# DCN-v2 cross layers on one core: 1024-row superblocks in 128x32 column tiles, the 32 leftover features packed four deep, and DMA transposes inside

## Chip, cores, metric

One core of a Trainium2 chip. The metric is the device time of one execution in microseconds (us), as a median over executions. The span, which the profile covers, runs from the first to the last instruction; the time is longer than the span. Engines are named as in the profile: PE is TensorE, PEld its weight loads, DVE VectorE, ACT ScalarE, POOL GpSimd, SP SyncE (it issues most of the DMAs here). "L200" is line 200 of the kernel in question.

## The reference

```python
B, D, L = 4096, 416, 6            # x0 [B, D], ws [L, D, D], bs [L, D], all bf16
def reference(x0, ws, bs):
    x = x0
    for l in range(L):
        x = x0 * (x @ ws[l] + bs[l]) + x
    return x
```

Every layer result is x0 times something: x_l = x0 * (1 + the sum of all earlier x @ w + b). Both kernels use this. PSUM keeps accumulating over the layers, the sum of the biases is prepared once (`cb_sb`), and an eviction is one instruction: (PSUM + bias) * x0. The width is 416 = 3 x 128 + 32, and the 32 leftover features are the awkward part.

## The kernel before

x0 is held transposed (features on partitions). Rows come in blocks of 512, two blocks (a pair) at a time, each with four PSUM banks. Per block and layer, TensorE does 12 full-array matmuls (4 output chunks x 3 input chunks, 512 columns each) and four 32-row tiles for the leftover input features. The leftover features are replicated four times, so the fourth output chunk is 128 columns wide like the other three (all 576 matmuls of L200 are `128*128` in the trace) but holds only 32 distinct results.

```python
for p in range(NPAIR):                       # 4 pairs of 512-row blocks
    emit_inT(p, 0)                           # 16 PE transposes of x0 per block into the block's own banks
    if p > 0:
        emit_inT(p, 1)
    for l in range(L):
        for par in range(2):
            ...                              # waits cut
            for m in range(NCH):             # NCH = 4 output chunks, the fourth is the leftover, 4 copies
                for k in range(3):
                    pe.matmul(ps[:, 4 * par + m, :],
                              lhsT=w_sb[:, l, k, m * 128:(m + 1) * 128],
                              rhs=src[:, k, cols], ...)
            for m in range(NCH):             # leftover input: four 32-row tiles side by side
                ins = pe.matmul(ps[:, 4 * par + m, :],
                                lhsT=w3_sb[32 * m:32 * m + 32, l, :],
                                rhs=src[32 * m:32 * m + 32, 3, cols],
                                tile_position=(32 * m, 0), ...)
            ins.then_inc(s_mm[par], 1)
    for par in range(2):
        pe.wait_ge(s_x[par], p * L + L)      # last layer evicted
        ...                                  # 16 PE transposes back per block, then ScalarE copies, then the store
# VectorE, per block and layer: four times
dve.scalar_tensor_tensor(out=xT_sb[:, c, cols], in0=ps[:, 4 * par + c, :],
                         scalar=cb_sb[:, c, l:l + 1], in1=x0T_sb[:, c, cols],
                         op0=ALU.add, op1=ALU.mult)
```

## Time and profile before

| | before |
|---|---|
| time, median of 2 runs | 199.01 us (198.84 to 199.18) |
| span of the profiled execution | 193.8 us |
| PE busy / DVE busy | 174.1 us / 130.8 us |
| one 512-row block and layer | 3.02 us (6.05 us per 1024 rows) |
| turn between two pairs | 9.2, 8.3 and 8.5 us |

In all the profile blocks below, rows of the view left out between two shown are marked by "...". The page of before: busy time and its share of the span, then two rows in 40 slices of the span (tenths of a slice that PE was busy, and tenths of full clock granted to it), and the chain of work that ended last, by engine.

```profile
PE 174.1 (90%) x1028; PEld 78.4 (40%) x1028; DVE 130.8 (68%) x192; ACT 31.8 (16%) x69; POOL 11.6 (6%) x50
...
PE   0595999999799999999969999999978999999971
...
PEclk9999999999958999999987999999997999999995
...
PE 84%; ACT 6%; DVE 5%; DMA 1%; issue 1%; SPq 1%; DVEq 0%; ACTq 0%
```

TensorE is the bound, and there are three dips, at which its granted clock falls too. The chain of before in order of time (start us, length us, what) has one of them in full:

```profile
46.79 2.70 PE ps L200 x12
49.49 0.36 PE ps L209 x4
...
49.87 2.73 DVE xT_sb L245 x4
...
52.65 2.34 PE ps L226 x16
54.99 1.83 PE ps L171 x16
...
56.84 2.07 ACT x0T_sb L269 x4
...
59.05 2.87 PE ps L200 x12
```

The regular part is 2.70 + 0.33 us. The turn, from 49.85 to 59.05, is a queue in which each step waits for the one before: last evictions, transposes out, transposes in, copies. Over 49 to 60 us the clock granted was 0.69; in the regular part it was 1.00.

### The profile page before, as it was taken

Reading aid. Unit: us, or ns where it says so; the run is one execution under the profiler, and the core shown is the slowest. Engines: PE = TensorE matmul, PEld = TensorE weight load, DVE = VectorE, ACT = ScalarE, POOL = GpSimd, SP = SyncE. Lnnn points to the kernel's source line nnn. Section 1 sums busy time; section 2 is a strip of 40 time slices with the busy share of each in tenths; the row PEclk is TensorE's granted clock in tenths of the full one; section 3 lists DMA queues with packets and bytes.
Section 4 is the critical chain, followed back from the end, with each engine's and each line's share of the span. In section 5 each row is a group of like instructions: output and inputs, shape, how many; then the busy total and the mean of one; then the engine's idle time right before and its main releaser. Section 6 shows DMA issues by size and latency. Waiting matters only on the chain.

```text
span 193.8 us, 2464 instructions
## 1 busy us (share of the span) xinstructions
PE 174.1 (90%) x1028; PEld 78.4 (40%) x1028; DVE 130.8 (68%) x192; ACT 31.8 (16%) x69; POOL 11.6 (6%) x50
## 2 busy tenths in 40 slices
PE   0595999999799999999969999999978999999971
PEld 0342434334374343433455434334356343343440
DVE  0023889898701988989820889898850698988970
ACT  2503000000365000000078000000049000000033
POOL 4176400000000000000000000000000000000000
PEclk9999999999958999999987999999997999999995
DMA  4699400000031000000022000000013000000005
GB/s 131 159 364 354 133 0 3 0 0 3 0 116 60 5 0 0 0 0 3 0 88 90 3 0 0 0 0 3 0 61 115 0 3 0 2 0 0 3 0 176
DMA packets 12411, 9.09 MB, mean 47 GB/s; under 512 B 1898, under 2 KB 12400, under 8 KB 12400
## 3 DMA queue, kind: packets, MB, share of 16 engines
q1 hardware_dynamic: 12400, 8.94, 14.7%
q8 instruction: 8, 0.13, 0.3%
q14 instruction: 3, 0.02, 0.0%
HBM read 5.53 MB, written 3.41 MB: 46 GB/s over the span
## 4 chain that ended last, share of the span: by engine, by line
PE 84%; ACT 6%; DVE 5%; DMA 1%; issue 1%; SPq 1%; DVEq 0%; ACTq 0%
PE ps L200 68%; PE ps L209 8%; DVE xT_sb L245 5%; PE ps L171 4%; ACT x0T_sb L269 4%; PE ps L226 4%; ACT o_sb L279 2%; DMA bsa_sb<-in_bs_dram 1%; DVEq L33 0%; SPq L73 0%; SPq L71 0%; SPq L70 0%; ACTq L33 0%; PE ps L154 0%
## 5 line engine op out<-in xcount | busy, mean ns | idle before, releaser
L245 DVE SCALAR_TENSOR_TENSOR xT_sb<-ps,cb_sb,x0T_sb 128x512 bf16<-128x512 f32 x192 | 130.8, 744 | 57.0 <-PE ps L209 57.0
L200 PE MATMUL ps<-xT_sb,w_sb 128*128 128x512 bf16 x480 | 110.6, 380 | 0.0
L200 PEld LDWEIGHTS ps<-xT_sb,w_sb 128*128 128x128 bf16 x480 | 43.7, 98 | 56.3 <-DVE xT_sb L245 6.8
L279 ACT ACTIVATE o_sb<-ps 128x416 bf16<-128x416 bf16 x32 | 14.0, 522 | 148.8 <-PE ps L226 148.8
L200 PE MATMUL ps<-x0T_sb,w_sb 128*128 128x512 bf16 x96 | 23.5, 397 | 5.2 <-ACT x0T_sb L269 5.1
L226 PE MATMUL ps<-ident,xT_sb 128*128 128x128 bf16 (+1 forms) x128 | 13.9, 223 | 5.1 <-DVE xT_sb L245 5.1
L269 ACT ACTIVATE x0T_sb<-ps 128x512 bf16<-128x512 bf16 x32 | 16.4, 613 | 7.2 <-PE ps L171 7.0
L200 PEld LDWEIGHTS ps<-x0T_sb,w_sb 128*128 128x128 bf16 x96 | 9.1, 101 | 17.4 <-issue 8.8
L209 PE MATMUL ps<-xT_sb,w_sb 32*128 32x512 bf16 x160 | 15.8, 384 | 0.0
L171 PE MATMUL ps<-ident,xin_sb 128*128 128x128 bf16 x128 | 13.7, 293 | 0.7 <-ACT o_sb L279 0.4
L226 PEld LDWEIGHTS ps<-ident,xT_sb 128*128 128x128 bf16 (+1 forms) x128 | 8.7, 99 | 10.8 <-DVE xT_sb L245 6.4
L171 PEld LDWEIGHTS ps<-ident,xin_sb 128*128 128x128 bf16 x128 | 11.9, 136 | 1.7 <-issue 1.6
L209 PEld LDWEIGHTS ps<-xT_sb,w_sb 32*128 32x128 bf16 x160 | 4.0, 90 | 17.0 <-issue 17.0
L132 POOL COPY xin_sb<-xin_sb 128x128 bf16<-128x128 bf16 x24 | 6.2, 296 | 8.2 <-DMA xin_sb<-in_x_dram 8.2
L154 PE MATMUL ps<-u_sb,bsa_sb 7*128 7x6 bf16 x4 | 0.2, 162 | 4.6 <-DMA bsa_sb<-in_bs_dram 4.6
L141 POOL COPY w_sb<-w_sb 128x96 bf16<-128x96 bf16 x18 | 4.1, 270 | 2.3 <-DMA w_sb<-in_ws_dram 2.1
L209 PE MATMUL ps<-x0T_sb,w_sb 32*128 32x512 bf16 x32 | 3.2, 384 | 0.0
L209 PEld LDWEIGHTS ps<-x0T_sb,w_sb 32*128 32x128 bf16 x32 | 0.8, 90 | 3.4 <-issue 3.4
L154 PEld LDWEIGHTS ps<-u_sb,bsa_sb 7*128 7x128 bf16 x4 | 0.2, 99 | 4.5 <-issue 4.5
L259 ACT ACT_TABLE_LOAD x1 | 1.3, 1283 | 0.8 <-PEq L298 0.8
L259 ACT ACTIVATE cb_sb<-ps 128x6 f32<-128x6 f32 x4 | 0.4, 181 | 2.8 <-PE ps L154 2.8
L118 POOL MEMSET bsa_sb<- 1x512 bf16 x1 | 0.5, 518 | 0.0
(7 smaller groups left out, 1.1 us busy)
## 6 DMA issues: line engine op xcount, KB each, us to landing
xin_sb<-in_x_dram SPq DMA_DIRECT2D x8, 416.0 KB, 7.0
out_dram<-o_sb SPq DMA_DIRECT2D x7, 416.0 KB, 2.7
w_sb<-in_ws_dram SPq DMA_DIRECT2D x6, 312.0 KB, 4.5
out_dram<-o_sb SPq DMA_DIRECT2D x4, 104.0 KB, 1.8
w_sb<-in_ws_dram SPq DMA_DIRECT2D x3, 48.0 KB, 2.5
w_sb<-in_ws_dram SPq DMA_DIRECT2D x4, 12.0 KB, 1.8
bsa_sb<-in_bs_dram SPq DMA_DIRECT2D x3, 0.4 KB
bsa_sb<-in_bs_dram SPq DMA_DIRECT2D x1, 4.9 KB
```

The lines of the kernel that those rows point to most:

```text
L118: pool.memset(bsa_sb[0:1, :], 1.0).then_inc(s_setup, 1)
L132: pool.tensor_copy(out=xin_sb[:, p * SUB:(p + 1) * SUB, DF + r * DR:DF + (r + 1) * DR], in_=xin_sb[:, p * SUB:(p + 1) * SUB, DF:D],).then_ ...
L141: pool.tensor_copy(out=w_sb[:, l, :, DF + r * DR:DF + (r + 1) * DR], in_=w_sb[:, l, :, DF:D],).then_inc(s_wr[l], 1)
L154: ins = pe.matmul(ps[:, 7, c * 8:c * 8 + L], lhsT=bsa_sb[:, c * 128:(c + 1) * 128], rhs=u_sb[:, :], start=True, stop=True,)
L171: ins = pe.transpose(out=psT[:, 4 * par + c, j * 128:(j + 1) * 128], in_=xin_sb[:, blk * SUB + j, c * 128:(c + 1) * 128], identity=ident[: ...
L200: pe.matmul(ps[:, 4 * par + m, :], lhsT=w_sb[:, l, k, m * 128:(m + 1) * 128], rhs=src[:, k, cols], start=(l == 0 and k == 0), stop=False, ...
L209: ins = pe.matmul(ps[:, 4 * par + m, :], lhsT=w3_sb[32 * m:32 * m + 32, l, :], rhs=src[32 * m:32 * m + 32, 3, cols], start=False, stop=Tru ...
L226: ins = pe.transpose(out=psT[:, 4 * par + j, c * 128:c * 128 + fw], in_=xT_sb[0:fw, c, b0:b0 + 128], identity=ident[0:fw, 0:fw],)
L245: ins = dve.scalar_tensor_tensor(out=xT_sb[:, c, cols], in0=ps[:, 4 * par + c, :], scalar=cb_sb[:, c, l:l + 1], in1=x0T_sb[:, c, cols], op ...
L259: ins = act.activation(out=cb_sb[:, c, :], in_=ps[:, 7, c * 8:c * 8 + L], func=ACTF.Copy)
L269: ins = act.activation(out=x0T_sb[:, c, cols], in_=psT[:, 4 * par + c, 0:NB], func=ACTF.Copy,)
L279: ins = act.activation(out=o_sb[:, blk * SUB + j, :], in_=psT[:, 4 * par + j, 0:D], func=ACTF.Copy,)
```

## The change

The intent is threefold. Pack the leftover so that TensorE streams less: its output in four row groups, side by side in four column tiles. Make the turns vanish: inner superblocks get their transposed input from DMA and give their output to DMA. Take the leftover's eviction off VectorE. Everything except the leftover's input runs in 128x32 column tiles, so that the array changes its tiling only twice per layer. The core of it, cut:

```diff
-    NB = 512
+    SB = 1024
+    NS = B // SB
+    H = SB // 2
+    G = SB // 4
+    TAIL, SPARE = 6, 7
 ...
+            # SP: input of superblocks 1 to 3, output of superblocks 0 to 2
+            for s in range(1, NS):
+                sp.dma_start_transpose(
+                    x0T_sb[:, :, s * SB:(s + 1) * SB], x0[s * SB:(s + 1) * SB, 0:DF]
+                ).then_inc(s_x0T[s], 16)
+            for s in range(NS - 1):
 ...
+                for c in range(NC):
+                    sp.dma_start_transpose(
+                        o_sb[:, s * JS:(s + 1) * JS, c * 128:(c + 1) * 128], xo_sb[:, s, c, :]
+                    ).then_inc(s_oT, 16)
+                sp.wait_ge(s_xt, n)
+                sp.dma_start_transpose(ot_sb[:, s, :, :], xot_sb[:, s, :]).then_inc(s_ot, 16)
 ...
+            # PE: the main product of a half (512 rows), 3 x 3 groups of four column tiles
+                                for q in range(4):
+                                    f0 = m * 128 + 32 * q
+                                    ins = tile_mm(
+                                        ps[32 * q:32 * q + 32, NC * half + m, :],
+                                        w_sb[:, l, k, f0:f0 + 32], src[:, k, o:o + H], q,
+                                        l == 0 and k == 0 and half == 0, True,
+                                    )
 ...
+            # PE: main(0, ...), then the leftover's input in row tiles; row groups g share banks in pairs; the batches keep two of one bank apart
+                    for i, jobs in enumerate((
+                        ((0, 0), (1, 1), (2, 0), (3, 1)), ((0, 2), (2, 2)),
+                        ((0, 1), (1, 0), (2, 1), (3, 0)), ((1, 2), (3, 2)),
+                    )):
+                        if i >= 2:
+                            pe.wait_ge(s_row, 3 * n + i - 1)
 ...
+            # PE: the leftover's output, one 256-row group per column tile, then main(1, None)
+                    for k in range(NC):
+                        for g in range(4):
+                            tile_mm(
+                                ps[32 * g:32 * g + 32, TAIL, 0:G], w_sb[:, l, k, DF:D],
+                                src[:, k, off + g * G:off + (g + 1) * G], g, l == 0 and k == 0, True,
+                            )
 ...
+            # ACT, then POOL: the leftover's eviction and product
+                    act.activation(
+                        out=t32_sb[:, n % 2, :], in_=ps[:, TAIL, 0:G], func=ACTF.Identity,
+                        bias=cb_sb[:, NC, l:l + 1],
+                    ).then_inc(s_ta, 1)
+                    pool.tensor_tensor(
+                        out=dst, in0=t32_sb[:, n % 2, :], in1=x0t_sb[:, s, :], op=ALU.mult
+                    ).then_inc(s_xt, 1)
```

In all, the first half superblock is still transposed by TensorE, as is the output of the last superblock. Twenty filler matmuls at the start are meant to bring TensorE to its full rate before the first product (in after they do not: its groups start 0.427 us apart, later ones 0.216; see run 9).

## The prediction

> **What bounds before.** TensorE. The chain of waits is 84% PE; the table of busy time has PE 90% (174.1 us), DVE 68% (130.8 us). The timeline shows a steady rhythm: each 512-row block and layer takes 3.02 us (12 full-array matmuls 2.70 us, then four 32-row tiles 0.33 us for 32 leftover features), so 6.05 us per 1024 rows, 145 us for 48. DVE fits inside (four evictions 2.73 us, 0.683 us apart). The rest of the chain is not rhythm: three block-pair turns of about 9 us each (49.9 to 59.1: last eviction, 32 transposes, ScalarE copies, nothing overlapping), about 27 us; start to the first main matmul 8.9 us; end after the last matmul 8.7 us (185.1 to 193.8). Time minus span is 5.2 us.
>
> **What the change does, per 1024 rows and layer.**
> - Main product: 18 groups of four 128x32 tiles, 512 columns. If the four run together, 18 x 0.216 = 3.89 us (0.216: the twelve matmuls, 2.70 us, less about 0.11 us for the mode switch; an estimate).
> - Leftover input in four row tiles at N=256, ordered in four batches, two of which wait for earlier ones. Estimate 0.71 us, from the 0.384 us of one 512-column tile less half its streaming, about 0.28 us, plus 0.43 us of queueing.[...]
> - Leftover output packed by four row groups in column tiles: 16 matmuls of 256 columns, four deep, about 0.43 us.
> - PE sum 5.2 us against 6.05. DVE: 6 evictions instead of 8, 6 x 0.683 = 4.1 us; the loop DVE, then ordered row tiles, then DVE is 4.1 + 0.75 + about 0.2 = 5.05 us, nearly a tie. The leftover's eviction moves to ScalarE (about 0.5 us) and GpSimd (estimate 0.6-1.2 us, from 0.296 us for a 128-wide copy); its result is due about 4 us later, so hidden. Rhythm: 5.3 us; 24 x 5.3 = 127 us. Gain 18 us.
> - Turns: input and output transposes of the inner superblocks go to DMA, and the next superblock's first layer depends on nothing just finished. Gain about 27 us, nearly all on the critical path.
> - Start and end remain: first layer done at about 14.5 us; end about 6.3 us.
>
> 14.5 + 23 x 5.3 + 6.3 = 143 us of span, + 5.2 = 148; I add 4 us for stalls in the first layers. **Predicted 152 us, range 143 to 168.** Faster by over 2%: 0.93; within: 0.04; slower: 0.03.
>
> **What shows each step.** Right: groups of four tiles 0.21-0.23 us apart in the timeline; rhythm per layer 5.2-5.5 us; no PE gap over 0.5 us at superblock borders; GpSimd never the releaser of PE; DVE busy about 105 us; final part 6-7 us.
>
> **What would make it wrong.**
> - [...]If weight loads of small tiles stop hiding[...].
> - DMA transposes slow: under about 60 GB/s (estimate, 851 KB in 14 us) the GpSimd tail copy waits and stalls the tail, and the first transpose delays layers 0 and 1.
> - Evictions at 0.744 us each instead of 0.683, plus slower ordered tiles: rhythm 5.7 us, 160 us.

The sum of 5.2 us for TensorE came from 3.89 + 0.43 us and 0.85 to 0.9 us for the row tiles. The last had, on top of the 0.71 us that the text derives, 0.14 to 0.19 us for a change of mode; that came to 5.17 to 5.22 us. The term is cut, as no trace showed it in that form, and the terms still printed make 5.03 us.

## The result, and the profile after

| | before | after |
|---|---|---|
| time, median of 2 runs | 199.01 us | 141.44 us (141.40, 141.47) |
| span of the profiled execution | 193.8 us | 138.9 us |
| PE / DVE busy | 174.1 / 130.8 us | 131.3 / 98.7 us |
| 1024 rows and one layer | 6.05 us | 5.13 us |
| turns | 26.0 us in all | none |

The ratio is 0.713, with a 95% interval of 0.704 to 0.722. Ratios here are the mean time of one kernel's runs over that of the other's of the same rounds, so they are not quite the ratio of the medians quoted (for this first result the two medians give 0.711). Executions over 1.5% slower than the fastest of the same kernel are left out of the means. The direction was forecast; the time lies 1.6 us under the lower end of the range.

The page of after, the same lines as of before:

```profile
PE 131.3 (94%) x2506; PEld 67.2 (48%) x2506; DVE 98.7 (71%) x149; ACT 17.7 (13%) x36; POOL 21.1 (15%) x44
...
PE   6799999999999999999999999999999999999950
...
PEclk9999999999999999999999999999999999999995
...
PE 90%; DVE 3%; DMA 3%; ACT 1%; SPq 0%; issue 0%
```

The dips are gone and so are those of the clock. The chain of after in order of time, from the first main product into the second layer, and across the border of superblocks 0 and 1 (the row tiles at 36.76 are those of superblock 0's last layer, at 41.89 those of superblock 1's first):

```profile
6.08 4.08 PE ps L174 x33
...
10.18 0.39 ACT x0t_sb L377
...
10.71 0.76 PE ps L272 x12
11.47 4.43 PE ps L174 x88
...
36.76 0.69 PE ps L272 x12
37.45 4.43 PE ps L174 x88
41.89 0.69 PE ps L272 x12
```

The border cannot be told from the rest: 4.43 + 0.69 us, layer after layer, with no wait between (in layers 2 to 4 of superblock 0 the first is 4.55 us, because eight transposes of the next leftover inputs run there). The timeline of one layer (start, length, engine, line, operation, shapes, count, and in brackets the idle time before it):

```profile
62.33 0.76 PE L272 MATMUL ps<-xt_sb,wt_sb 32*128 32x256 bf16 x12
...
63.02 0.51 PE L174 MATMUL ps<-xT_sb,w_sb 128*32 128x256 bf16 x12
63.13 4.04 DVE L348 SCALAR_TENSOR_TENSOR xT_sb<-ps,cb_sb,x0T_sb 128x512 bf16<-128x512 f32 x6 [1.09 <-PE ps L272]
...
63.36 0.28 PE L174 MATMUL ps<-xt_sb,wc_sb 128*32 128x256 bf16 x4
...
63.47 4.06 PE L174 MATMUL ps<-xT_sb,w_sb 128*32 128x512 bf16 x72
63.70 0.47 ACT L387 ACTIVATE t_sb<-ps,cb_sb 128x256 f32<-128x256 f32 x1 [4.65 <-PE ps L174]
64.25 0.67 POOL L158 TENSOR_TENSOR xt_sb<-t_sb,x0t_sb 128x256 bf16<-128x256 f32 x1 [4.46 <-ACT t_sb L387]
...
67.46 0.76 PE L272 MATMUL ps<-xt_sb,wt_sb 32*128 32x256 bf16 x12
```

Row tiles start at 62.33 and again at 67.46: the rhythm is 5.13 us. The leftover's result leaves GpSimd at 64.92 and is due at 67.46. VectorE finishes its six evictions at 67.17, only 0.29 us before the row tiles that must wait for it. In the single instructions of the trace, the groups of four 512-column tiles start 0.216 us apart, those of 256 columns 0.11 us.

Where the 54.9 us of span went, by subtraction on the two chains: turns 26.0 us (9.20 + 8.31 + 8.46); rhythm 24 x (6.05 - 5.13) = 22.1 us. The remaining 6.8 us are start and end (first products, and the second block's transposes and copies in the middle of the first pair of before).

### The profile page after: what moved, and what is told of

The parts are those of the page before. It is cut to its first block, busy times and chain, and to the rows that moved or that the text cites. A ratio compares the mean times of both kernels' runs of the same rounds, so it can differ in the third digit from the quotient of the medians.

```text
span 138.9 us, 5386 instructions
## 1 busy us (share of the span) xinstructions
PE 131.3 (94%) x2506; PEld 67.2 (48%) x2506; DVE 98.7 (71%) x149; ACT 17.7 (13%) x36; POOL 21.1 (15%) x44
## 4 chain that ended last, share of the span: by engine, by line
PE 90%; DVE 3%; DMA 3%; ACT 1%; SPq 0%; issue 0%
PE ps L174 77%; PE ps L272 12%; DVE xo_sb L348 3%; DMA xin_sb<-in_x_dram 3%; PE ps L312 1%; PE ps L198 1%; ACT o_sb L403 1%; SPq L90 0%; ACT x0t_sb L377 0%
## 5 line engine op out<-in xcount | busy, mean ns | idle before, releaser
L348 DVE SCALAR_TENSOR_TENSOR xT_sb<-ps,cb_sb,x0T_sb 128x512 bf16<-128x512 f32 x120 | 80.9, 743 | 26.1 <-PE ps L272 26.1
L174 PE MATMUL ps<-xT_sb,w_sb 128*32 128x512 bf16 (+1 forms) x1680 | 91.1, 364 | 0.0
L174 PEld LDWEIGHTS ps<-xT_sb,w_sb 128*32 128x32 bf16 x1680 | 42.9, 97 | 37.2
L158 POOL TENSOR_TENSOR xt_sb<-t_sb,x0t_sb 128x256 bf16<-128x256 f32 x20 | 13.5, 674 | 86.3 <-ACT t_sb L387 86.3
L387 ACT ACTIVATE t_sb<-ps,cb_sb 128x256 f32<-128x256 f32 x24 | 11.4, 474 | 103.0 <-PE ps L174 103.0
L174 PE MATMUL ps<-x0T_sb,w_sb 128*32 128x512 bf16 (+1 forms) x336 | 20.4, 389 | 0.0
L348 DVE SCALAR_TENSOR_TENSOR xo_sb<-ps,cb_sb,x0T_sb 128x512 bf16<-128x512 f32 x24 | 16.2, 744 | 4.3 <-PE ps L272 4.3
L272 PE MATMUL ps<-xt_sb,wt_sb 32*128 32x256 bf16 x240 | 15.2, 274 | 0.0
L174 PEld LDWEIGHTS ps<-x0T_sb,w_sb 128*32 128x32 bf16 x336 | 9.0, 101 | 8.4 <-issue 1.6
L158 POOL TENSOR_TENSOR xot_sb<-t_sb,x0t_sb 128x256 bf16<-128x256 f32 x4 | 2.7, 674 | 17.8 <-ACT t_sb L387 17.8
L198 PE MATMUL ps<-ident,xin_sb 128*128 128x128 bf16 x12 | 1.6, 305 | 1.1 <-DMA xin_sb<-in_x_dram 1.1
```

The lines of the kernel that those rows point to most:

```text
L158: pool.tensor_tensor(out=dst, in0=t32_sb[:, n % 2, :], in1=x0t_sb[:, s, :], op=ALU.mult).then_inc(s_xt, 1)
L174: return pe.matmul(dst, lhsT=lhsT, rhs=rhs, start=start, stop=stop, skip_group_check=True, tile_position=(0, 32 * q),)
L198: ins = pe.transpose(out=psT[:, NC * (1 - h) + c, (j % 2) * 128:(j % 2 + 1) * 128], in_=xin_sb[:, j, c * 128:(c + 1) * 128], identity=iden ...
L272: ins = pe.matmul(ps[:, NC * (g // 2) + m, (g % 2) * G:(g % 2) * G + G], lhsT=wt_sb[p, l, m * 128:(m + 1) * 128], rhs=srct[p, :], start=l ...
L348: dve.scalar_tensor_tensor(out=dst, in0=ps[:, NC * half + c, :], scalar=cb_sb[:, c, l:l + 1], in1=x0T_sb[:, c, o:o + H], op0=ALU.add, op1= ...
L387: act.activation(out=t32_sb[:, n % 2, :], in_=ps[:, TAIL, 0:G], func=ACTF.Identity, bias=cb_sb[:, NC, l:l + 1],).then_inc(s_ta, 1)
```

## Experiments

Two theories stood for each part. Mine was that streaming in TensorE is the whole of the rhythm, and that the leftover's packing, not the column tiles, shortened it; that the turns were removed whole; and that the prediction was high because of terms added for safety and for time outside the span. The rivals are named in each text.

The base is the changed kernel's 141.44 us, and for runs 6 to 12 its repetition in run 5 (runs 9 to 12 were in other rounds than run 5). Runs 1 to 4 were on one chip, 5 to 12 on another. "Expected" is the text before each run.

### 1. The main product in full-array matmuls again

```diff
-                                for q in range(4):
-                                    f0 = m * 128 + 32 * q
-                                    ins = tile_mm(ps[32 * q:32 * q + 32, NC * half + m, :],
-                                        w_sb[:, l, k, f0:f0 + 32], src[:, k, o:o + H], q, ...)
+                                ins = pe.matmul(ps[:, NC * half + m, :],
+                                    lhsT=w_sb[:, l, k, m * 128:(m + 1) * 128], rhs=src[:, k, o:o + H], ...)
```

> The changed kernel with the 18 main groups per layer as full 128x128 matmuls again, everything else kept. Theory (the gain of the rhythm is not from column tiles, they only save one mode switch per layer: column-row-column has two, full-row-column-full has three): rhythm 5.13 to about 5.25-5.35 us, time 141.4 to 144-147 us. Rival (small column tiles themselves stream faster, or their weight loads hide better): rhythm over 5.5 us, time over 150 us.[...]

Measured: 144.25 us (143.21 to 144.44). In its timeline the row tiles start at 63.25 and 68.48, a rhythm of 5.23 us:

```profile
63.25 0.76 PE L271 MATMUL ps<-xt_sb,wt_sb 32*128 32x256 bf16 x12
...
64.28 0.28 PE L174 MATMUL ps<-xt_sb,wc_sb 128*32 128x256 bf16 x4
64.49 3.57 PEld L228 LDWEIGHTS ps<-xT_sb,w_sb 128*128 128x128 bf16 x18 [0.21 <-issue]
64.49 4.06 PE L228 MATMUL ps<-xT_sb,w_sb 128*128 128x512 bf16 x18
...
68.48 0.76 PE L271 MATMUL ps<-xt_sb,wt_sb 32*128 32x256 bf16 x12
```

Eighteen full-array matmuls take 4.06 us, exactly what 72 column tiles take in the line of after. So four tiles abreast stream like one full matmul (0.216 us from one to the next in both traces), and their four weight loads stay hidden (in the layer of after at 63.36 the 72 loads are 3.67 us of PEld, over the 4.06 us of the matmuls). The 0.10 us per layer lies ahead of the full matmuls, where the array changes from column tiles to the whole: they start 0.21 us after the leftover's last group (64.28), while in after the same step takes 0.11 us (63.36 to 63.47). Avoiding that switch is worth 24 x 0.10 = 2.4 us of the 2.8 us that column tiles brought by the time (3.6 us by the median span, 142.25 against 138.65); the rest is not accounted for.

### 2. The kernel before, only its turns removed

```diff
+            for p in range(2, NBLK):                      # SP: blocks 2 to 7
+                sp.dma_start_transpose(x0T_sb[:, 0:3, p * NB:(p + 1) * NB], x0[p * NB:(p + 1) * NB, 0:DF])
+                sp.wait_ge(s_xr[p], 3)
+                sp.dma_start_transpose(x0T_sb[:, 3, ...], xrep_sb[:, p * SUB:(p + 1) * SUB, :] ...)
 ...                                                       # output of blocks 0 to 5 likewise, a GpSimd copy for the leftover
-                emit_inT(p, 0)
-                if p > 0:
-                    emit_inT(p, 1)
+                if p == 0:
+                    emit_inT(p, 0)
```

> The kernel before with one part of the change alone: its three inner turns use DMA transposes in and out (512-row blocks, full-array and 32-row matmuls, tail on VectorE all as before). Theory (the turns held 26 us of the critical path and DMA transposes take all of it away, the rhythm of 3.02 us is untouched): 199.0 to 172-175 us, no PE gap over 0.5 us at the block-pair borders. Rival (the turn gain needs the 1024-row superblocks, or DMA transposes bring waits of their own): over 180 us.

Measured: 172.36 us against 199.04 us in the same rounds, 26.7 us less, by the medians of all executions. Some of both kernels were slow; the fast ones alone have means of 170.85 and 197.85 us, 27.0 us less (ratio 0.864, 0.850 to 0.877). The chain of this run, across the border of its first two pairs (which begins at 53.99 with the second pair's first layer):

```profile
53.66 0.33 PE ps L250 x4
53.99 2.70 PE ps L241 x12
```

The turns are gone with 512-row blocks too, and the rhythm of 3.02 us is untouched. So this part alone is worth almost half the gain, and it needs neither superblocks nor tiles. It is the DMA transposes, and the fact that a pair's first layer then waits for nothing but its own banks.

### 3. The leftover's output unpacked

```diff
                         for g in range(4):
-                            tile_mm(ps[32 * g:32 * g + 32, TAIL, 0:G], ..., g, l == 0 and k == 0, True)
+                            for q in (range(4) if s > 0 else (g,)):
+                                tile_mm(ps[32 * q:32 * q + 32, TAIL if q == g else SPARE, 0:G], ..., q, ...)
```

> The changed kernel with the packing of the leftover output undone in 18 of the 24 layers (superblocks 1 to 3): each of the four 256-row groups again occupies all four column tiles, three of the four results go to an unused bank; result stays right. 36 more matmuls of 256 columns per layer, four abreast[...]. Theory (the rhythm is bound by streaming in TensorE, and the packing is nearly the whole 0.92 us that the rhythm gained): rhythm 5.13 to about 6.09 us in those layers, time 141.4 to about 158.7 us (157-160). Rival (slack elsewhere in the layer hides part of it): under 153 us.

Measured: 158.7 us (157.97 to 158.92), result right. The chain has 5.42 us where after has 4.43, again with the row tiles' 0.69:

```profile
60.27 5.42 PE ps L174 x124
65.69 0.69 PE ps L272 x12
```

That is 0.99 us more for 36 more matmuls, nine groups of four that start 0.11 us apart in the trace (the expected 6.09 us was 5.13 + 0.96 us for the nine); in 18 layers it makes 17.8 us by the rhythm, and 17.3 us were measured by the time. Nothing hides any of it. Before, the fourth output chunk streamed 2 x 3 x 512 columns per 1024 rows, of which this packing leaves 3 x 256; so the packing accounts for the 0.92 us of the rhythm, with what little the row tiles and the corner add and take.

### 4. The row tiles without their order (wrong result)

```diff
-                        ((0, 0), (1, 1), (2, 0), (3, 1)), ((0, 2), (2, 2)),
-                        ((0, 1), (1, 0), (2, 1), (3, 0)), ((1, 2), (3, 2)),
+                        ((0, 0), (1, 1), (2, 0), (3, 1)), ((0, 0), (1, 1), (2, 0), (3, 1)),
+                        ((0, 0), (1, 1), (2, 0), (3, 1)),
 ...
-                        if i >= 2:
-                            pe.wait_ge(s_row, 3 * n + i - 1)
```

> Wrong result on purpose: the twelve row-tile matmuls of the leftover input write one bank per row group, so that no two row groups share a bank and the two ordering waits go; three batches of four instead of four batches. Theory (the order costs time in every layer: 4 batches and a wait, 0.69 us from batch start to the next mode): 0.69 to about 0.43-0.50 us, time 141.4 to 135-137 us. Rival ([...]VectorE's loop takes over): over 140 us.

Measured: 135.78 us (135.33 to 136.12). In the chain the row tiles fall from 0.69 to 0.44 us:

```profile
55.48 4.44 PE ps L174 x88
59.92 0.44 PE ps L270 x12
```

So the order costs 0.25 us per layer, 5.7 us in all. The starts of the batches in the two traces divide it: in after the third batch starts 0.24 us after the second, here 0.11 us, so the first wait is about half; the other half is the fourth batch, which is 0.12 us after the third. The order is the largest thing left in the rhythm besides streaming. Whether the waits could go in the right kernel was not tried: that would take away the waits between row groups that share a bank, not the sharing, and no run shows what becomes of the result then. It stays open.

### 5. The changed kernel once more

> The changed kernel once more, on the same chip as the next three runs, as their base. All theories: 141-142.5 us; time minus span 2.0-2.8 us, as in every run so far, so that the 5.2 us taken in the prediction was the median of two runs set against the span of a faster run and not a fixed cost.

Measured: 141.54 us median (139.18 to 141.94, four runs). The times confirm the first ones. Time minus span was 1.98 to 3.34 us, wider than expected. For the kernel before, over the 25 executions of the three sets of rounds, it was 2.05 to 2.14 us, while the spans themselves went from 193.9 to 197.7 us. So the 193.8 us of the first profile was one of the shortest executions and the 199.01 us came from others: the 5.2 us were 2.1 us of fixed time and about 3.1 us of scatter between executions. Of this run's four executions the one of 139.18 us was labelled fast and the others slow, because they lie over 1.5% above it; their clocks (0.989 to 0.999, against 0.990) are at most 0.001 lower, and their spans, 138.6 to 138.8 us against 137.2, are those of the first runs. So they serve as the base: 141.54 us of time, 138.65 us of median span. By the labels alone the base would be the one execution of 139.18 us, runs 6 to 8 would stand 2.4 us further above it, and runs 9 to 12 (139.83, 139.47, 140.89 and 138.99 us) would gain nothing. So those small effects rest on what the traces show and not on the times. In most other runs time minus span was 1.7 to 2.0 us, so part of a difference in time from this base (mean 2.7 us) lies outside the span; for effects of about 1 us the span is the steadier measure, and both are given below.

### 6. The inner output transposes done twice

```diff
                 for c in range(NC):
+                    sp.dma_start_transpose(od_sb[:, c, :, :], xo_sb[:, s, c, :]).then_inc(s_oT, 16)
+                sp.wait_ge(s_oT, 32 * NC * s + 16 * NC)
+                for c in range(NC):
                     sp.dma_start_transpose(
```

> The changed kernel with every inner output DMA transpose done twice, one after the other (first into a scratch tile). Theory (the DMA transposes are wholly off the critical path, with several us to spare before GpSimd's copy is due): no change, within 0.5 us of the base. Rival (they are near the limit, as the prediction allowed with its 4 us for stalls): over 2 us slower, with PE waiting for GpSimd in the second or third layer of superblocks 1 to 3.

Measured: 141.92 us against 141.54; by median span 139.95 against 138.65. By the time it is within the expected 0.5 us (one of its four executions, 143.47 us, was slow; the fast ones are 141.28 to 141.96); by the span it is 1.3 us slower, so the theory's "no change" did not hold, and what the rival named, PE waiting for GpSimd, is seen, though the loss is 1.3 us and not over 2. The waits of this run (engine, line, waited for whom: us in total, times, longest) and its timeline after superblock 0 say how:

```profile
PE ps L278 <- POOL xt_sb L164: 1.3, 2, 1.1
```

```profile
56.79 0.40 POOL L172 COPY o_sb<-ot_sb 128x256 bf16<-128x256 bf16 x1 [7.76 <-DMA ot_sb<-xot_sb]
...
57.87 0.76 PE L278 MATMUL ps<-xt_sb,wt_sb 32*128 32x256 bf16 x12 [1.10 <-POOL xt_sb L164]
```

With twice the transposes the leftover lands at about 56.8, and PE waits 1.1 us. In the changed kernel its transpose is issued at 46.64 and lands 2.4 us later (the median of these), at about 49.0. It would be in time until about 55.7. The slack at this border is thus about 6.6 us (an estimate across two runs): the way of failure that the prediction named is real and is 6.6 us away. From the first issue (41.62) to this landing the DMA transposes of superblock 0's output in after (832 KB) went at some 115 GB/s (the prediction put its danger under about 60), and SP's four issues alone took 6.2 us of those 7.4; the transfer by itself was not measured.

### 7. The leftover on VectorE again

```diff
+                        if half == 1:                     # VectorE, between its two halves
+                            dve.wait_ge(s_to, n + 1)
+                            dve.scalar_tensor_tensor(out=..., in0=ps[:, TAIL, 0:G], scalar=cb_sb[:, NC, l:l + 1],
+                                in1=x0t_sb[:, s, :], op0=ALU.add, op1=ALU.mult).then_inc(s_xt, 1)
 ...                                                       # the ScalarE and GpSimd instructions of it removed
```

> The changed kernel with the leftover's eviction and product on VectorE again (one 128x256 instruction per layer between its two halves) in place of ScalarE and GpSimd. Theory (VectorE's loop is almost tied with TensorE: its last eviction must be done before the next ordered row tiles, with about 0.3 us to spare, although it idles 1.1 us per layer): rhythm 5.13 to 5.25-5.4 us, 3 to 6 us slower. Rival (1.1 us idle swallows 0.42 us): within 0.7 us of the base.

Measured: 146.04 us (145.94 to 146.72), 4.5 us slower (5.4 us by the median span). The row tiles of its timeline:

```profile
58.71 0.76 PE L266 MATMUL ps<-xt_sb,wt_sb 32*128 32x256 bf16 x12 [0.18 <-DVE xT_sb L351]
...
59.51 2.07 DVE L351 SCALAR_TENSOR_TENSOR xT_sb<-ps,cb_sb,x0T_sb 128x512 bf16<-128x512 f32 x3 [0.94 <-PE ps L266]
...
64.09 0.76 PE L266 MATMUL ps<-xt_sb,wt_sb 32*128 32x256 bf16 x12 [0.19 <-DVE xT_sb L351]
```

The leftover's instruction takes 0.48 us (L336 in the same timeline; the rival had put it at 0.42). The rhythm is 5.38 us, and now PE waits for VectorE, although VectorE still idles 0.94 us per layer. That idle time cannot be used: it is the time in which it waits for the row tiles. Busy shares (71% in after) hide that a loop of two engines is nearly closed.

### 8. The last superblock's output by DMA as well

```diff
-            for s in range(NS - 1):
+            for s in range(NS):                           # SP's DMA transposes and stores
 ...                                                       # PE's last transposes, their copies and four stores removed
```

> The changed kernel with the last superblock's output also by DMA transposes, as the inner ones. Theory (TensorE transposes are the faster way where nothing is left to hide the DMA: 5 us from the last eviction to the end now, against four transposes in turn, a copy and one 832 KB store): 5 to 9 us slower, all of it after the last eviction. Rival (DMA transposes are as good): within 2 us.

Measured: three fast runs of 146.51 to 147.09 us, 5 us slower (6.2 us by the median span of the three, 144.9 us). A fourth execution took 225.17 us at a mean granted clock of 0.571: its trace records 0.56 of full clock from 9.3 to 214.1 us. None of the other 55 executions of the experiments' kernels did so, and nothing here explains it. The profile fell on that execution; only its end is used, in which TensorE has no part:

```profile
211.29 0.75 DVE L325 SCALAR_TENSOR_TENSOR xo_sb<-ps,cb_sb,x0T_sb 128x512 bf16<-128x512 f32 x1 [0.36 <-PE ps L174]
212.12 3.99 SPq L110 DMA_TRANSPOSE o_sb<-xo_sb  x3
216.15 1.24 SPq L114 DMA_TRANSPOSE ot_sb<-xot_sb  x1
```

From the last eviction's end (212.04) to the end of the span (223.4) are 11.4 us; in after they are 5.0 (133.86 to 138.9). The 6.4 us between are about what the fast executions lost in span. Here, where nothing is left to hide a DMA, TensorE's transposes are the shorter way. The exception in the change is right.

### 9 to 12. Can start and end be shortened?

```diff
# 9: more filler
-    NFILL = 20
+    NFILL = 29
+                if h == 0:
+                    for i in range(4):
+                        pe.matmul(ps[:, SPARE, 0:128], lhsT=ones_sb[:, :], rhs=ones_sb[:, :], start=True, stop=True)
# 10: 9, and tail_transposes(0) moved into the middle of the first main(0)
# 11: after without 9 and 10; in the last layer one eviction of six by ScalarE and GpSimd, last transposes chunk by chunk
+                            for c in range(NC):
+                                pe.wait_ge(s_xb, NC * (n - 1) + c + 1)
# 12: 10 and 11 together
```

> The changed kernel with more filler matmuls ahead of the input transposes (29 instead of 20, and 4 between the two halves), so that TensorE does not idle before the first product. Theory (the first product's eight or nine groups ran at 0.43 us each, half speed[...]; kept busy it reaches full clock earlier): first product about 2 us instead of 3.3-3.8 us, 1-2 us faster (139.5-140.5 us). Rival (the clock rises at a time that the filler does not move): within 0.5 us of 141.5.

Measured: 139.83 us (139.19 to 140.2), 1.7 us less; but by median span 137.85 against 138.65, only 0.8 us less, and the single spans overlap (137.2 to 138.2 here, 137.2 to 138.8 in run 5), so the time alone decides nothing. The input transposes and the first product of after and of this run, from their timelines in that order:

```profile
4.12 0.80 PE L198 MATMUL ps<-ident,xin_sb 128*128 128x128 bf16 x6 [0.75 <-DMA xin_sb<-in_x_dram]
5.26 0.82 PE L198 MATMUL ps<-ident,xin_sb 128*128 128x128 bf16 x6 [0.33 <-DMA xin_sb<-in_x_dram]
...
6.21 3.81 PE L174 MATMUL ps<-x0T_sb,w_sb 128*32 128x512 bf16 x36
```

```profile
4.13 0.77 PE L198 MATMUL ps<-ident,xin_sb 128*128 128x128 bf16 x6
...
5.91 2.13 PE L174 MATMUL ps<-x0T_sb,w_sb 128*32 128x512 bf16 x36
...
18.16 0.30 PE L174 MATMUL ps<-ident,xtl_sb 128*32 128x128 bf16 x8 [0.76 <-DMA xtl_sb<-in_x_dram]
```

The filler closes the two idle stretches before the product (0.75 and 0.33 us), and the product's groups then start 0.216 us apart instead of 0.427. The clock records in the packed traces say when the clock opened: the first one at full clock begins at 4.68 us in this run, 3.6 us after the filler's start at 1.06 us, and at 9.66 us in after, which is where the spacing changes too. (PEclk of the page and of `--windows` reads 1.00 before that only because the trace has no record there yet, so it cannot be used for the start.) In the nine profiles of the changed kernel and its variants with the old filler it opened at 7.88 to 9.66 us, in run 9 at 4.68, in run 10 at 4.78, but in run 12 at 6.97. So the rival falls: the filler does move the time. It does not fix it, and whether closing the gaps or the longer filler did it was not separated. The first row tiles start at 8.80 us, against 10.71 in after (10.19 in run 5). The last line shows where part of that went: in the second layer TensorE is now early for the leftover input of the next superblock, and waits 0.76 us for its DMA. In after the same transposes started at 18.92 us without a wait. The slow first product had hidden the loads.

> As the run before, and the leftover's first input transposes moved into the middle of the first product, so that ScalarE's copy is done when the row tiles are due (PE waited 0.6 us for it, and the transposes took 0.25 us). Theory: another 0.5-0.9 us, 138.8-140 us. Rival (the leftover's input arrives too late): no further change.

Measured: 139.47 us (139.14 to 139.71), median span 137.45: 0.4 us less than run 9 by either, short of the expected 0.5 to 0.9 and within the scatter of run 9's own executions. If it is real, it did not come from where it was meant to come: the first row tiles started at 9.01 us, not before the 8.80 of run 9. In run 9 they wait for GpSimd's copies of a weight corner, which had themselves waited 5.2 us for their DMA, and here too those copies end (8.91) just before the row tiles start. So ScalarE was, by the timeline, no longer what they waited for. The 0.76 us wait of run 9 in the second layer is not there in this run's profile; that is a load that landed earlier, which the edit did not aim at.

> The changed kernel with its end shortened: in the last layer one of VectorE's six evictions goes to ScalarE and GpSimd, and the last transposes follow each eviction instead of waiting for all three. Theory (after the last row tiles the chain is six evictions 4.05 us, twelve transposes 0.86 us, copy, store): 0.68 + about 0.5 us, 140.2-140.6 us. Rival (GpSimd's two-input product of 512 columns, 1.3 us, delays the leftover and gives it back): no change or slower.

Measured: 140.89 us (140.41 to 141.82) against 141.54; but by the span 138.85 against 138.65, no gain. The chain of waits showed evictions, transposes and a copy as the end. VectorE does finish earlier, yet the end does not move. Two views of after, and then the same two of this run (ScalarE's and SP's timelines):

```profile
134.13 0.39 ACT L397 ACTIVATE o_sb<-ps 128x256 bf16<-128x256 bf16 x1
134.55 1.97 SPq L125 DMA_DIRECT2D out_dram<-o_sb  x4
```

```profile
133.92 0.39 ACT L425 ACTIVATE o_sb<-ps 128x256 bf16<-128x256 bf16 x1
134.33 1.96 SPq L127 DMA_DIRECT2D out_dram<-o_sb  x4
```

The four last stores are issued one after the other, 0.49 us each in the mean, and the first waits for ScalarE's copy of the leftover, which stands third in ScalarE's queue. So in after the fourth could not be issued before 134.55 + 3 x 0.49 = 136.02 us, later than ScalarE's last copy (135.59), which the page's chain follows. GpSimd's product of 512 columns took 1.16 us (1.3 us expected), and one of 256 columns 0.67 us (both in this run). My theory of the end was wrong; doing the leftover's copy first would be the next thing to try, and was not run.

> Start and end of the two runs before together: 137.8-139.3 us if the effects add, as they lie at opposite ends of the chain.

Measured: 138.99 us (138.86 to 139.92; ratio to before 0.706), inside the expected range and the fastest correct kernel here: 2.5 us under the changed kernel by the time, 1.4 us by the span (137.25 against 138.65). These are differences from a base of other rounds. The start earned it: run 10 alone, in the same rounds, has 137.45, so the end added next to nothing.

## Why the prediction was right or wrong

Right in kind, wrong in size: 152 us was forecast with a range from 143, and 141.44 us came. Point by point:

- **TensorE bounds both kernels.** Right. Run 3 adds nine groups of 0.11 us to a layer, and the layer grows by 0.99 us.
- **Turns, 27 us, nearly all critical.** Right: 26.0 us by the chain, 27.0 us by the fast executions of run 2.
- **Main product 3.89 us, leftover output 0.43 us, row tiles 0.85 to 0.9 us with a change of mode, sum 5.2 us.** Nearly right: the sum measured 5.13 us. Groups start 0.216 us apart, so eighteen take 3.89 us, as forecast; the change of mode after them adds 0.1 us (the row tiles start 0.32 us after the last group). The leftover's output took 0.45 us (63.02 to 63.47) and the row tiles 0.69 us (62.33 to 63.02), 0.79 us with the change, against the forecast 0.85 to 0.9. That changes of mode cost time shows in before as well: 0.311 us from the last full matmul to the row tiles, 0.216 us between full ones. The fear that small weight loads stop hiding did not come true (0.216 us with four small loads or one large, run 1).
- **Rhythm 5.3 us.** Slightly wrong. I rounded 5.2 up for the near tie with VectorE. The tie is real (0.29 us, run 7), but a tie not lost costs nothing: here the layer took the larger of the two loops, not a little more. From the end of the first layer at 13.79 us to the end of the last main product at about 132.1 us, 23 layers took 118.3 us, not 121.9: 3.6 us.
- **"I add 4 us for stalls in the first layers."** Wrong: the chain shows none after the first layer. Its end, put at 14.5 us, was 13.79. The danger was not imaginary: with a faster start the second layer does wait for a load (run 9).
- **"+ 5.2", time minus span.** Wrong. It was taken as fixed, and is 2.1 us in every execution of before and was 2.6 and 2.8 us in the two first runs of after. The profile of before was of a short execution and the median of longer ones (run 5). This is an error of about 2.6 us in the sum.
- **End 6.3 us.** It was 6.8 us, 0.5 us the other way.

Of the signs that the prediction listed, the spacing of groups (0.216 us), the borders without a gap, GpSimd never releasing PE after the fillers, and the final part (6.8 us) came as listed; the rhythm (5.13) and VectorE's busy time (98.7) came in below it.

The sum closes: 152 - 3.6 - 4.0 - 2.6 - 0.7 + 0.5 = 141.6 us, against 141.47 of the profiled execution. The step that failed is therefore the last line of the prediction, "14.5 + 23 x 5.3 + 6.3 = 143 us of span, + 5.2 = 148; I add 4 us for stalls". All three of its loose terms, the rhythm rounded up, the stall allowance and the fixed 5.2 us, erred in the same direction, and the lower end of the range (143) left no room for that. The mechanisms were not at fault: three terms were mis-sized. The rhythm was 5.14 us a layer over those 23 layers (5.13 in the regular part) and not 5.3, no stall was measured after the first layer where 4 us had been added, and the time outside the span 2.6 us and not 5.2. Two of them were margins of safety, so it is no accident that they lay on the same side; the third came from setting two executions against each other.

What stays open: why the kernel before varies by 3.8 us of span between executions; why time minus span of the kernels after varies from 1.7 to 3.3 us; the one execution at about half clock in run 8; and whether the row tiles' order could do without its waits.

## What to carry to other kernels

Count what is between the regular parts before tuning the regular part: here taking DMA for the transposes at three borders was worth 27 us, more than the 22 us of the whole gain in rhythm. A fixed cost taken as time minus span is only good if both numbers come from the same execution, and allowances for fear belong in the range, not in the sum. Before shortening a start or an end, look for the second chain beside it: the loads behind a slow first product, the serial issue of the last stores behind the last copies.
